# Beacon attention followed by a two-layer MoE block: another order of work in the first two batches

## The chip, the core and the metric

The kernel runs on one core of a Trainium2 chip. Its engines run side by side: TensorE (PE; its weight loads are shown as PEld) multiplies matrices, VectorE (DVE) and ScalarE (ACT) work on elements, GpSimd (POOL) does copies and issues loads, and SyncE (SP) issues loads and stores. Each engine takes its instructions in the order in which they are written, and waits where an operand or a buffer isn't ready. The metric is the device time of one execution in microseconds; lower is better.

## The reference

Eight batches (B), eight heads (H), 576 queries (S) of width 64 (D), and 16 beacon keys in front of the 576 ordinary ones. All queries see the beacon keys; the ordinary keys are causal. The attention output of a batch, heads side by side, gives 576 rows of width 512, and all 4608 rows go through two matrices with a leaky ReLU between them.

```python
k_all = np.concatenate([beacon_k, k], axis=2)
v_all = np.concatenate([beacon_v, v], axis=2)
scores = scale * np.matmul(q, k_all.transpose(0, 1, 3, 2))
causal[:, Nb:] = np.triu(np.ones((S, S), dtype=bool), k=1)
scores = np.where(causal, -1000000000.0, scores)
...
a /= a.sum(-1, keepdims=True) + 1e-09
attn_out = np.matmul(a, v_all)
...
x = attn_out.transpose(0, 2, 1, 3).reshape(B * S, H * D)
h = x @ w_in
g = np.maximum(0.01 * h, h)
out = g @ w_out
```

## The kernel before

**Pairs.** Heads are worked in pairs: four pairs per batch, 32 in all, numbered g = 0 to 31. Each pair has these parts, in this order of need:

- `load_qk(b, grp)` (L124): q and k of two pairs (half a batch), four loads issued by GpSimd, which turn the type to bf16. `permute` (L157) is a copy on GpSimd that brings each 128 x 1152 half into the order that the transposes want. The first pair's own half comes over SP and ACT instead.
- `t_q(g, which)` (L229): nine transposes on TensorE into PSUM (line 244), and one copy out of it (line 249) into qT or kT. For kT a small copy puts the beacon keys in front (L239).
- `score(g, n)` (L256) for n = 0 to 3: the causal blocks of the scores, computed transposed (keys on partitions) into one of two PSUM buffers `sc` (matmuls, L267), and their exponential on ScalarE into `aT` (L278, and L282 for the last block of 80 rows). There are three `aT`, two qT and two kT.
- `masks(g)` (L290): three multiplications on VectorE (L292, L299, L305) that clear the diagonal blocks.
- `value(g, half)` (L314): 12 matmuls for the first three blocks of queries, 18 for the last two (L333); the column of ones in `v_aug` gives the sum. VectorE takes its reciprocal (L342) and multiplies (L343) into `x_nat`.
- `finish(g)` (L488): five transposes of `x_nat` (L355) and a copy into `xT` (L360), which the MoE part reads. After the fourth pair of a batch, one more chunk of 512 rows is ready (`ready`; after the last batch all nine).

**Values.** `load_v(b)` (L207) issues six loads from SP into one of two raw buffers; the first pair's q and k lie in the first of them, so batch 1's values go there once these were read. `cast_v` (L222) turns a batch's values into bf16 in five casts, on VectorE for batches 0 and 1, on GpSimd later. `behind(a, b)` (L199) makes load a wait until load b has landed.

**MoE.** `fill()` (L401) emits the next piece: either `moe1`, four matmuls of 512 columns (L369) with the leaky ReLU on ScalarE (L376), for one of the 16 column blocks of a chunk, or a quarter of `moe2`, four matmuls (L385); after the fourth quarter VectorE copies out (L394) and SP stores. The two kinds take turns where both can run; a chunk's moe2 needs all its 16 moe1. There are 288 fills. If no chunk is ready, `fill()` emits nothing. The weights come in four loads each (`load_w_in`, `load_w_out`, 512 KB each as stored), issued by GpSimd; block i of w_in serves four moe1.

**PSUM.** All tiles other than the scores (transposes, values, MoE accumulators) take turns in four buffers of one tag ("one"), each waiting for the copy out of the tile four before it.

**Order.** The order on every engine is the one written out (`manual_schedule`). The loop over g (L496) emits, per iteration: scores 0 and 1 of pair g, `finish(g - 3)`, `value(g - 2, 0)`, the transposes of pair g + 1, scores 2 and 3 of pair g, `value(g - 2, 1)`, `masks(g)`; so values are two pairs behind scores, and the transposes of x three. Between these stand eight slots for fills: none for g below 6, four for g = 6 and 7, all from g = 9. Iteration 8 is written out apart: it finishes pairs 5 to 7 with fills between, puts 16 fills behind them, and then starts pairs 8 and 9.

Before the loop stand the first loads, the permutes of batch 0, the load of batch 1's q and k behind the last load of v0, and a warm-up of 24 matmuls. The weights are loaded in iteration 3, behind v1. The cast of v0 stands in iteration 2, that of v1 in iteration 5; the transposes of the beacon keys of batches 1 to 7 (L187, which need the cast of `bk` on GpSimd, L178) in iteration 2.

Of the kernel before, what the change touches and what calls it, by code (L numbers as in the profile page):

```python
# [15 lines left out]
def kernel(  # L16
# [11 lines left out]
    nc = tc.nc  # L28

    B, H, S, D = q.shape  # L30
# [5 lines left out]
    NPAIR = H // 2  # L36
# [73 lines left out]
    def load_w_in(i):  # L110
        return nc.gpsimd.dma_start(
            out=w_in_sb[:, :, i * 512 : (i + 1) * 512], in_=w_in_r[:, :, i * 512 : (i + 1) * 512]
        )

    def load_w_out(i):
        return nc.gpsimd.dma_start(
            out=w_out_sb[:, i * 4 : (i + 1) * 4, :], in_=w_out_r[:, i * 4 : (i + 1) * 4, :]
        )
# [5 lines left out]
    def load_qk(b, grp):  # L124


        qk_raw[b, grp] = (
            qkpool.tile([128, 2, RI, D], BF16, name="q_raw"),
            qkpool.tile([128, 2, RI, D], BF16, name="k_raw"),
        )  # L130
        first = None
        for e in range(2):
            if b == 0 and grp == 0 and e == 0:
                continue
            h0 = 4 * grp + 2 * e
            for src, dst in zip((q, k), qk_raw[b, grp]):
                dma = nc.gpsimd.dma_start(  # L137
                    out=dst[e * RP : (e + 1) * RP],
                    in_=src[b, h0 : h0 + 2].rearrange("h (p i) d -> p h i d", i=RI),
                )  # L140
                first = first or dma
        return first
# [14 lines left out]
    def permute(b, grp, which, copy, p0=0, p1=128):  # L157

        if (b, grp) not in nat:
            nat[b, grp] = (  # L160
                natpool.tile([128, RI, 2, D], BF16, name="q_nat"),
                natpool.tile([128, RI, 2, D], BF16, name="k_nat"),
            )
        src, dst = qk_raw[b, grp][which], nat[b, grp][which]
        if b == 0 and grp == 0 and p0 == 0:
            src = first_raw[which]
        copy(out=dst[p0:p1], in_=src[p0:p1].rearrange("p h i d -> p i h d"))  # L167
# [9 lines left out]
    def cast_beacon_k(b0, b1, copy):  # L177
        copy(  # L178
            out=bk[:, b0:b1],
            in_=bk_raw[:, b0:b1, None, :].to_broadcast([128, b1 - b0, 2, D]),  # L180
        )
# [17 lines left out]
    def behind(ins, other):  # L199
        tc.add_manual_dep(  # L200
            ins.ins,
            other.ins.name,
            mybir.DependencyInfo(mybir.DependencyClass.Sync, mybir.DependencyReason.DATA),
            reason="loads in order of need",
        )

    def load_v(b, after=None):  # L207

        t = rawpool.tile([128, NKB, H, D], FP32, name="v_raw")
        v_raws[b] = t  # L210
        first = nc.sync.dma_start(out=t[0:NB, 0], in_=beacon_v[b].rearrange("h p d -> p h d"))
        if after is not None:
            behind(first, after)
        nc.sync.dma_start(out=t[NB:128, 0], in_=v[b, :, 0:112].rearrange("h p d -> p h d"))
        for c in (1, 2, 3, 4):
            last = nc.sync.dma_start(  # L216
                out=t[0 : ROWS[c], c],
                in_=v[b, :, OFF[c] : OFF[c] + ROWS[c]].rearrange("h p d -> p h d"),
            )
        return last  # L220
# [194 lines left out]
    def warm_up(n):  # L415

        ps = ps_one.tile([128, 512], FP32, name="av", tag="one")
        for i in range(n):
            nc.tensor.matmul(out=ps[:, 0:128], lhsT=ident, rhs=ident, start=True, stop=True)

    NG = B * NPAIR

    def has(g):
        return 0 <= g < NG
# [10 lines left out]
    with order:  # L435
        first = load_first_pair()
        load_qk(0, 0)
        make_identity(nc, ident)
        load_qk(0, 1)
        v0 = load_v(0, after=first)  # L440
        load_beacon_k(1, B, nc.sync)
        make_mask()
        make_ones()
        cast_beacon_k(0, 1, nc.scalar.copy)
        permute(0, 0, 0, nc.vector.tensor_copy, 0, RP)
        permute(0, 0, 1, nc.scalar.copy, 0, RP)
        for which in range(2):
            permute(0, 0, which, nc.gpsimd.tensor_copy, RP, 2 * RP)
        for which in range(2):
            permute(0, 1, which, nc.gpsimd.tensor_copy)  # L450
        behind(load_qk(1, 0), v0)
        v1 = load_v(1, after=v0)
        load_qk(1, 1)
        cast_beacon_k(1, B, nc.gpsimd.tensor_copy)
        warm_up(24)
        beacon_transposes(0, 1)
        t_q(0, 0)
        t_q(0, 1, nc.scalar.copy)

        def loads(g):  # L460
            b, hp = divmod(g, NPAIR)
            if g == 1:
                for which in range(2):
                    permute(1, 0, which, nc.gpsimd.tensor_copy)
            elif g == 3:
                for which in range(2):
                    permute(1, 1, which, nc.gpsimd.tensor_copy)
                behind(load_w_in(0), v1)
                for i in range(1, 4):
                    load_w_in(i)  # L470
                for i in range(4):
                    w = load_w_out(i)
                load_v(2, after=w)
                load_qk(2, 0)
                load_qk(2, 1)
            elif b >= 1 and b < B - 1:
                if b > 1:
                    if hp == 0:
                        load_v(b + 1)
                    if hp < 2:  # L480
                        load_qk(b + 1, hp)
                if hp >= 2:
                    for which in range(2):
                        permute(b + 1, hp - 2, which, nc.gpsimd.tensor_copy)
                if hp == 3:
                    cast_v(b + 1, nc.gpsimd)

        def finish(g):  # L488

            x_transposes(g)  # L490
            b, hp = divmod(g, NPAIR)
            if hp == NPAIR - 1:
                ready[0] = NCH if b == B - 1 else b + 1


        for g in range(NG + 3):  # L496
            if has(g):
                loads(g)
            slots = [0] * 8 if g < 6 else [0, 0, 1, 1, 0, 1, 1, 0] if g < 8 else [1] * 8

            def slot(n):
                if slots[n]:
                    fill()

            if g == 2 * NPAIR:

                finish(g - 3)
                value(g - 2, 0)
                fill()
                value(g - 2, 1)  # L510
                fill()
                value(g - 1, 0)
                finish(g - 2)
                value(g - 1, 1)
                fill()
                fill()
                finish(g - 1)
                for n in range(16):
                    fill()
                t_q(g, 0)  # L520
                t_q(g, 1)
                fill()
                fill()
                score(g, 0)
                score(g, 1)
                fill()
                fill()
                fill()
                t_q(g + 1, 0)
                t_q(g + 1, 1)  # L530
                score(g, 2)
                score(g, 3)
                fill()
                fill()
                masks(g)
                fill()
                continue

            late = g - 2 == 2 * NPAIR - 1 or g - 2 == 2 * NPAIR - 2
            if has(g):  # L540
                score(g, 0)
                score(g, 1)
            slot(0)
            if g == 2:
                cast_v(0, nc.vector)
            if g == NPAIR + 1:
                cast_v(1, nc.vector)
            if has(g - 3) and not 2 * NPAIR < g <= 2 * NPAIR + 2:
                finish(g - 3)
            slot(1)  # L550
            if has(g - 2) and not late:
                value(g - 2, 0)
            slot(2)
            slot(3)
            if has(g + 1) and g + 1 != 2 * NPAIR:
                t_q(g + 1, 0)
                t_q(g + 1, 1)
            if has(g):
                score(g, 2)
                score(g, 3)  # L560
            slot(4)
            if has(g - 2) and not late:
                value(g - 2, 1)
            slot(5)
            if g == 2:
                beacon_transposes(1, B)
            slot(6)
            if has(g):
                masks(g)
            slot(7)  # L570
        while done2[0] < NCH * NF:
            fill()

# [29 lines left out]
```

The softmax here doesn't subtract the row's maximum and nothing guards it: scores larger than these inputs give would overflow.

## Time and profile before

| | us |
|---|---|
| median of 13 runs | 379.1 (377.23 to 380.31) |
| profiled execution | 377.35 |
| its span | 375.6 |
| TensorE busy | 352.9 |
| ScalarE busy | 195.6 |
| VectorE busy | 171.4 |
| GpSimd busy | 102.5 |
| scores of pairs 0 to 7 start at | 8.91, 12.30, 15.89, 24.25, 30.48, 34.81, 40.55, 46.91 |
| last x transposes of batch 1 (12 fills done) | 58.50 |

The span is what the profile covers; the execution's own time is 1.75 us longer (377.35 against 375.6). Busy matmuls overlap, so a single matmul of 512 columns is shown with 379 ns, while four of them follow each other within 0.86 us; the starts tell more than the busy time. An arrow in a wait ("<-") names what released the engine. All times in the text count from the start of the span.

### The profile page before, as it was taken

How to read it: one execution, taken by the hardware profiler on the slowest of the kernel's cores; microseconds unless marked ns; L12 is line 12 of the kernel's file. 1: busy time of each engine (PE TensorE's matmuls, PEld its weight loads, DVE VectorE, ACT ScalarE, POOL GpSimd, SP SyncE). 2: the span in 40 equal slices, each digit the busy share in tenths (PEclk: the TensorE clock that was granted, in tenths of full speed). 3: DMA queues.
4: the chain of work that ended last, by engine and by line, in shares of the span. 5: the costliest groups of instructions: out<-in, count | busy, mean ns of one | idle time of the engine just before them, and what ended most of it. 6: DMA issues, size and time to landing. Idle time of an engine off the chain costs nothing.

```text
span 375.6 us, 7668 instructions
## 1 busy us (share of the span) xinstructions
PE 352.9 (94%) x3217; PEld 187.5 (50%) x3264; DVE 171.4 (46%) x402; ACT 195.6 (52%) x308; POOL 102.5 (27%) x143
## 2 busy tenths in 40 slices
PE   4869799999998899999999999999999999999996
PEld 4556464444555455555554555555554554444442
DVE  3768842253558645554456436644554332000021
ACT  3937674376436684368634763487336701643300
POOL 8579216685204812181208202300000000000000
PEclk9999999999999999999999999999999999999999
DMA  8997999959119910178015901100010011001012
GB/s 172 168 201 124 203 201 209 211 106 150 61 61 219 169 24 29 53 133 156 3 58 115 198 2 57 58 2 2 28 58 30 1 45 69 2 0 58 28 56 84
DMA packets 58371, 33.82 MB, mean 90 GB/s; under 512 B 41441, under 2 KB 53473, under 8 KB 58337
## 3 DMA queue, kind: packets, MB, share of 16 engines
q0 software_dynamic: 13152, 13.34, 22.7%
q1 hardware_dynamic: 44896, 19.67, 21.3%
q8 instruction: 25, 0.41, 0.4%
q10 hardware_dynamic: 288, 0.33, 0.3%
q14 instruction: 10, 0.07, 0.1%
HBM read 37.22 MB, written 9.44 MB: 124 GB/s over the span
## 4 chain that ended last, share of the span: by engine, by line
PE 85%; DVE 6%; DMA 3%; POOL 2%; issue 2%; SPq 1%; ACT 0%; POOLq 0%
PE acc L385 33%; PE acc L369 33%; PE av L333 7%; PE sc L267 6%; PE tp L244 4%; PE tp L355 2%; DMA v_raw<-in_k_dram 1%; DMA v_raw<-in_v_dram 1%; DVE osb L394 1%; DVE xT L360 1%; POOL k_raw L137 1%; SPq L216 1%; DVE x_nat L343 1%; DVE qT L249 1%; DVE kT L249 1%
## 5 line engine op out<-in xcount | busy, mean ns | idle before, releaser
L278 ACT ACTIVATE aT<-sc 128x928 bf16<-128x928 f32 (+2 forms) x128 | 102.4, 855 | 76.9 <-PE sc L267 76.7
L369 PE MATMUL acc<-xT,w_in_sb 128*128 128x512 bf16 x551 | 137.7, 379 | 3.5 <-DVE xT L360 2.1
L385 PE MATMUL acc<-w_out_sb,gT 128*128 128x512 bf16 x554 | 135.6, 379 | 1.5 <-issue 0.6
L376 ACT ACTIVATE gT<-acc 128x512 bf16<-128x512 f32 x144 | 85.7, 600 | 80.8 <-PE acc L369 79.6
L385 PEld LDWEIGHTS <-gT 128*128 128x128 bf16 x576 | 52.1, 98 | 60.0 <-issue 5.3
L369 PEld LDWEIGHTS <-w_in_sb 128*128 128x128 bf16 x576 | 52.3, 98 | 59.5 <-issue 4.1
L394 DVE COPY osb<-acc 128x512 f32<-128x512 f32 x36 | 24.8, 690 | 93.4 <-PE acc L385 92.9
L267 PE MATMUL sc<-qT,kT 64*128 64x128 bf16 (+5 forms) x384 | 42.5, 309 | 5.6 <-DVE kT L249 2.8
L333 PEld LDWEIGHTS <-aT 128*128 128x128 bf16 (+1 forms) x960 | 38.8, 100 | 16.7 <-issue 3.3
L333 PE MATMUL av<-v_aug,aT 128*128 128x65 bf16 (+1 forms) x960 | 41.9, 197 | 1.4 <-DVE xT L360 1.0
L167 POOL COPY q_nat<-q_raw 128x1152 bf16<-128x1152 bf16 (+1 forms) x16 | 18.5, 1156 | 82.4 <-PE tp L244 53.6
L249 DVE COPY qT<-tp 128x576 bf16<-128x576 bf16 x32 | 24.2, 755 | 33.0 <-PE tp L244 33.0
L343 DVE TENSOR_TENSOR x_nat<-av,rec 128x384 bf16<-128x384 f32 x64 | 31.4, 491 | 2.2
L225 POOL CAST v_aug<-v_raw 128x512 bf16<-128x512 f32 (+1 forms) x30 | 19.4, 684 | 33.0 <-PE av L333 31.5
L267 PEld LDWEIGHTS <-kT 64*128 64x128 bf16 (+1 forms) x384 | 18.3, 100 | 20.1 <-issue 11.5
L360 DVE COPY xT<-tp 128x576 bf16<-128x576 bf16 x32 | 14.5, 452 | 30.2 <-PE tp L355 30.1
L342 DVE RECIPROCAL rec<-av 128x6 f32<-128x6 f32 x64 | 11.9, 185 | 34.1 <-PE av L333 34.1
L137 POOL DMA_DIRECT2D k_raw<-in_k_dram x31 | 21.2, 683 | 7.8 <-DMA w_out_sb<-in_moe_w_out_dram 4.4
L249 DVE COPY kT<-tp 128x576 bf16<-128x576 bf16 x31 | 23.2, 749 | 0.0
L137 POOL DMA_DIRECT2D q_raw<-in_q_dram x31 | 19.5, 630 | 12.7 <-DMA v_raw<-in_v_dram 4.6
L299 DVE TENSOR_TENSOR aT<-aT,mask 128x768 bf16<-128x768 bf16 x32 | 21.6, 675 | 1.2 <-ACT aT L278 1.2
L167 POOL COPY k_nat<-k_raw 128x1152 bf16<-128x1152 bf16 (+1 forms) x16 | 18.5, 1157 | 1.7 <-DMA k_raw<-in_k_dram 1.5
(33 smaller groups left out, 147.4 us busy)
## 6 DMA issues: line engine op xcount, KB each, us to landing
out_dram<-osb SPq DMA_DIRECT2D x36, 256.0 KB, 2.0
v_raw<-in_v_dram SPq DMA_DIRECT2D x24, 256.0 KB, 6.1
q_raw<-in_q_dram POOLq DMA_DIRECT2D x31, 144.0 KB, 6.1
k_raw<-in_k_dram POOLq DMA_DIRECT2D x31, 144.0 KB, 6.4
w_in_sb<-in_moe_w_in_dram POOLq DMA_DIRECT2D x4, 512.0 KB, 8.6
w_out_sb<-in_moe_w_out_dram POOLq DMA_DIRECT2D x4, 512.0 KB, 16.7
v_raw<-in_v_dram SPq DMA_DIRECT2D x8, 224.0 KB, 4.7
v_raw<-in_v_dram SPq DMA_DIRECT2D x8, 160.0 KB, 4.9
```

The costliest lines, as they stand in the source:

```text
L137: dma = nc.gpsimd.dma_start(out=dst[e * RP : (e + 1) * RP], in_=src[b, h0 : h0 + 2].rearrange("h (p i) d -> p h i d", i=RI),)
L167: copy(out=dst[p0:p1], in_=src[p0:p1].rearrange("p h i d -> p i h d"))
L249: copy(out=dst.rearrange("c (p i) -> c p i", i=RI), in_=ps[:, 0:S].rearrange("c (i p) -> c p i", i=RI),)
L267: nc.tensor.matmul(out=sc[0 : ROWS[c], par, col - c0 : col - c0 + w], lhsT=kT[ps_, c * 128 : c * 128 + ROWS[c]], rhs=qT[ps_, q0 : q0 + w], ...
L278: last = nc.scalar.activation(out=aT[:, :, c0 : c0 + w], in_=sc[:, :, 0:w], func=AF.Exp, scale=0.125)
L299: nc.vector.tensor_tensor(out=diag, in0=diag, in1=tri[:, None, None, :].to_broadcast([128, 2, 3, 128]), op=ALU.mult,)
L333: nc.tensor.matmul(out=avv[:, n, 0 : D + 1], lhsT=aT[0 : ROWS[c], par, a0 : a0 + 128], rhs=va[0 : ROWS[c], c, 2 * hp + par, :], start=(c = ...
L343: nc.vector.tensor_tensor(out=x_nat[:, t0:t1].rearrange("p t e d -> p (t e) d"), in0=avv[:, :, 0:D], in1=rec[:, n0:n1, None].to_broadcast( ...
L369: nc.tensor.matmul(out=acc, lhsT=w_in_sb[:, j, fc * 128 : (fc + 1) * 128], rhs=xT[:, j, i * 512 : (i + 1) * 512], start=(j == 0), stop=(j ...
L376: nc.scalar.activation(out=gT[i][:, fc, :], in_=acc, func=AF.Prelu, alpha=0.01)
L385: nc.tensor.matmul(out=acc, lhsT=gT[i][:, fc, t * 128 : (t + 1) * 128], rhs=w_out_sb[:, fc, :], start=(fc == 0), stop=(fc == NF - 1),)
L394: nc.vector.tensor_copy(out=osb, in_=acc)
```

## The change

The loop is written anew for the first two batches (g < 8):

1. Within iteration g: scores 0 and 1, the transposes of pair g + 1, score 2, `value(g - 1, 0)`, score 3, `value(g - 1, 1)`, `finish(g - 1)`, `masks(g)`. So values follow one pair behind, and `finish` directly behind the values. (In iteration 1 the two halves of value 0 both stand behind score 3.)
2. For odd g the copy of the next pair's kT out of PSUM is on ScalarE.
3. The cast of v0 moves from iteration 2 to 1, that of v1 from iteration 5 to 4. The beacon transposes stay in iteration 2, ahead of the transposes of pair 3.
4. Fills: one at the end of iteration 4, four in each of iterations 5 to 7 (before: four in each of 6 and 7). Iteration 8 finishes pair 7 alone, with three fills ahead of that and 10 instead of 16 behind it.
5. From iteration 9 on the loop has the eight fills as before, but values are one pair behind instead of two, and `finish(g - 1)` stands at the end of the iteration, behind `masks(g)`. The loop ends two iterations sooner.
6. Loads: w_in(0) comes directly behind batch 1's first q and k; v1 waits for the first of these; q and k of pairs 6 and 7 wait for v1; the other weights follow them, ahead of the loop, and v2 behind the last weight. GpSimd permutes pairs 4 and 5 ahead of these waits. The loads of batch 2's q and k stay in iteration 3.

```diff
-        behind(load_qk(1, 0), v0)
-        v1 = load_v(1, after=v0)
-        load_qk(1, 1)
+        gate = load_qk(1, 0)
+        behind(gate, v0)
+        load_w_in(0)
+        v1 = load_v(1, after=gate)
         cast_beacon_k(1, B, nc.gpsimd.tensor_copy)
+        for which in range(2):
+            permute(1, 0, which, nc.gpsimd.tensor_copy)
+        behind(load_qk(1, 1), v1)
+        load_w_in(1)
+        load_w_in(2)
+        load_w_in(3)
+        for i in range(4):
+            w = load_w_out(i)
+        v2 = load_v(2, after=w)
...
         def loads(g):
             b, hp = divmod(g, NPAIR)
-            if g == 1:
-                for which in range(2):
-                    permute(1, 0, which, nc.gpsimd.tensor_copy)
-            elif g == 3:
+            if g == 3:
                 for which in range(2):
                     permute(1, 1, which, nc.gpsimd.tensor_copy)
-                behind(load_w_in(0), v1)
-                for i in range(1, 4):
-                    load_w_in(i)
-                for i in range(4):
-                    w = load_w_out(i)
-                load_v(2, after=w)
                 load_qk(2, 0)
                 load_qk(2, 1)
...
-        for g in range(NG + 3):
+        for g in range(NG + 1):
...
+            if g < 2 * NPAIR:
+
+                moe = g > NPAIR
+                score(g, 0)
+                score(g, 1)
+                if moe:
                     fill()
+                if g + 1 < 2 * NPAIR:
+                    if g + 1 == 3:
+                        beacon_transposes(1, B)
+                    t_q(g + 1, 0)
+                    t_q(g + 1, 1, nc.scalar.copy if g % 2 else nc.vector.tensor_copy)
+                score(g, 2)
+                if g == 1:
+                    cast_v(0, nc.vector)
+                if g == NPAIR:
+                    cast_v(1, nc.vector)
+                if g > 1:
+                    value(g - 1, 0)
+                    if moe:
+                        fill()
+                score(g, 3)
+                if g == 1:
+                    value(0, 0)
+                if g > 0:
+                    value(g - 1, 1)
+                    if moe:
+                        fill()
+                    finish(g - 1)
+                    if g >= NPAIR:
+                        fill()
+                masks(g)
+                continue
 
             if g == 2 * NPAIR:
 
-                finish(g - 3)
-                value(g - 2, 0)
-                fill()
-                value(g - 2, 1)
-                fill()
                 value(g - 1, 0)
-                finish(g - 2)
+                fill()
                 value(g - 1, 1)
                 fill()
                 fill()
                 finish(g - 1)
-                for n in range(16):
+                for n in range(10):
                     fill()
...
-            if has(g - 3) and not 2 * NPAIR < g <= 2 * NPAIR + 2:
-                finish(g - 3)
-            slot(1)
-            if has(g - 2) and not late:
-                value(g - 2, 0)
-            slot(2)
-            slot(3)
-            if has(g + 1) and g + 1 != 2 * NPAIR:
+            fill()
+            fill()
+            if g - 1 >= 2 * NPAIR:
+                value(g - 1, 0)
+            fill()
+            fill()
+            if has(g + 1):
                 t_q(g + 1, 0)
                 t_q(g + 1, 1)
             if has(g):
                 score(g, 2)
                 score(g, 3)
-            slot(4)
-            if has(g - 2) and not late:
-                value(g - 2, 1)
-            slot(5)
...
+            fill()
+            if g - 1 >= 2 * NPAIR:
+                value(g - 1, 1)
+            fill()
+            fill()
             if has(g):
                 masks(g)
-            slot(7)
+            if g - 1 >= 2 * NPAIR:
+                finish(g - 1)
+            fill()
```

More of the change, by code (lines that the diff above doesn't have):

```diff
@@ L493, in finish @@
                 ready[0] = NCH if b == B - 1 else b + 1
-        for g in range(NG + 3):
+        for g in range(NG + 1):
             if has(g):
                 loads(g)
-            slots = [0] * 8 if g < 6 else [0, 0, 1, 1, 0, 1, 1, 0] if g < 8 else [1] * 8
-            def slot(n):
-                if slots[n]:
-                    fill()
+            if g < 2 * NPAIR:
[3 more added lines that the diff above has]
+                if moe:
+                    fill()
+                if g + 1 < 2 * NPAIR:
[24 more added lines that the diff above has]
+                continue
             if g == 2 * NPAIR:
-                finish(g - 3)
-                value(g - 2, 0)
+                value(g - 1, 0)
                 fill()
-                value(g - 2, 1)
-                fill()
-                value(g - 1, 0)
-                finish(g - 2)
                 value(g - 1, 1)
@@ L537 @@
                 continue
-            late = g - 2 == 2 * NPAIR - 1 or g - 2 == 2 * NPAIR - 2
             if has(g):
@@ L542 @@
                 score(g, 1)
[L543 to L547, printed above, removed]
-            if has(g - 3) and not 2 * NPAIR < g <= 2 * NPAIR + 2:
-                finish(g - 3)
-            slot(1)
-            if has(g - 2) and not late:
-                value(g - 2, 0)
-            slot(2)
-            slot(3)
-            if has(g + 1) and g + 1 != 2 * NPAIR:
+            fill()
+            fill()
+            if g - 1 >= 2 * NPAIR:
+                value(g - 1, 0)
+            fill()
+            fill()
+            if has(g + 1):
                 t_q(g + 1, 0)
@@ L560 @@
                 score(g, 3)
-            slot(4)
-            if has(g - 2) and not late:
-                value(g - 2, 1)
-            slot(5)
-            if g == 2:
-                beacon_transposes(1, B)
-            slot(6)
+            fill()
[3 more added lines that the diff above has]
+            fill()
             if has(g):
                 masks(g)
-            slot(7)
+            if g - 1 >= 2 * NPAIR:
+                finish(g - 1)
+            fill()
         while done2[0] < NCH * NF:
```

## The prediction

> **What bounds the kernel now.** I read the page first (busy shares, then the slices), then the stretches of 10 us, the waits of TensorE before 90 us, and the timelines of TensorE, VectorE and GpSimd.
>
> ```profile
> PE 352.9 (94%) x3217; PEld 187.5 (50%) x3264; DVE 171.4 (46%) x402; ACT 195.6 (52%) x308; POOL 102.5 (27%) x143
> ...
> PE   4869799999998899999999999999999999999996
> ```
>
> TensorE is the bound from slice 6 on; only the head and slices 12 and 13 have holes. The stretches show the head and that second hole:
>
> ```profile
> 20.00:30.00 10.00, 7.00 (x87) 5.17 (x85) 6.60 (x16) 4.23 (x6) 6.94 (x10) 1.00 1.09 192
> 30.00:40.00 10.00, 7.39 (x141) 5.51 (x138) 9.20 (x27) 7.72 (x13) 8.41 (x11) 1.00 0.87 138
> ...
> 110.00:120.00 10.00, 9.08 (x138) 5.70 (x138) 7.03 (x17) 5.90 (x8) 2.24 (x2) 1.00 0.88 187
> 120.00:130.00 10.00, 8.35 (x102) 4.74 (x101) 7.11 (x18) 7.21 (x13) 8.62 (x14) 1.00 1.04 181
> ```
>
> After the length, the columns are busy PE, PEld, DVE, ACT, POOL. In the head TensorE isn't only idle, it is slow: nine transposes take
>
> ```profile
> 26.98 0.66 PE L244 MATMUL tp<-ident,q_nat 64*128 64x64 bf16 x9 [0.44 <-POOL q_nat L167]
> ...
> 32.47 0.43 PE L244 MATMUL tp<-ident,q_nat 64*128 64x64 bf16 x9
> ```
>
> and four score matmuls 1.00 at 30.48 and 0.62 at 34.81, so the array turned to full rate near 32 us, after 4 us without a gap (28.1 to 32.1); the clock row doesn't show it. The second hole is a lack of MoE work:
>
> ```profile
> 109.98 0.58 PE L267 MATMUL sc<-qT,kT 64*128 64x512 bf16 x4
> ...
> 123.62 0.38 PE L369 MATMUL acc<-xT,w_in_sb 128*128 128x512 bf16 x1 [1.01 <-DVE xT L360]
> ...
> 131.12 0.59 PE L267 MATMUL sc<-qT,kT 64*128 64x512 bf16 x4
> ```
>
> The scores of pairs 12 and 15 (pair 11's start at 100.17), and between them a first fill that waits for xT. VectorE, and then GpSimd, which the edits load anew:
>
> ```profile
> 36.08 1.96 DVE L225 CAST v_aug<-v_raw 128x512 bf16<-128x512 f32 x5
> ```
>
> ```profile
> 16.05 0.61 POOL L137 DMA_DIRECT2D q_raw<-in_q_dram  x1 [4.61 <-DMA v_raw<-in_v_dram]
> ...
> 22.32 1.01 POOL L178 CAST bk<-bk_raw 128x896 bf16<-128x896 f32 x1
> ```
>
> The casts of v1 are VectorE's longest single block; GpSimd's queue stands still until v0 has landed, and the beacon cast comes behind its loads.
>
> [...] at 37.96 the copy of xT starts as the five casts end, and TensorE had waited 0.97 for it. [...] some 200 GB/s in all from 22 to 29 us with both issuing.
>
> **The change part by part.** Pairs are numbered 0 to 31 over all batches; times of before are starts in the timeline of TensorE. Units at full rate: a fill is 0.8625 (16 matmuls in 3.45 in the chain of waits); a pair's attention 2.91 (9.81 from scores 11 to 12, less 8 fills).
>
> Transposes between score groups: in batch 0 they stood there already. What really moves is the value part, from two pairs behind to one, and the transposes of x, from three behind to directly after the value's second half. They now see the normalization, 0.18 + 0.42 on VectorE with its handovers 0.85, with nothing on TensorE beside it in iterations 1 to 4 (from 5 on a fill of 0.86 stands there and covers it).
>
> *Pairs 0 to 2.* Pair 0 is as before (8.91, 12.30). Pair 1 needs value 0, so the cast of v0, whose last load lands at 16.05: casts end 16.5, value at half rate 0.98 + 1.17 to 18.65, normalization to 19.55, transposes to 20.05. Scores of pair 2 begin there (before 15.89), and end at 21.0. The transposes of the other beacon keys wait for GpSimd's cast: four issues from 16.05 to 20.0, w_in(0) 0.77, cast 1.0, so 21.85. The two stalls of before there (2.06 until 23.38, and 0.49 + 0.44 at pair 4's q and k) nearly vanish: a cover gained, not lost. Then beacon 0.9, q and k 1.0, scores and values 0.5 + 0.98 + 0.5 + 1.15 to 26.95, normalization, transposes: pair 3 starts at 28.3 (before 24.25, with its values two pairs further behind; in work the two are level).
>
> *Pair 3*: scores 0.95, q and k 1.0, 0.5, 1.0, 0.4 to 32.1. I let the array turn to full rate there, as before. 0.57 + 0.85 + 0.3: pair 4 at 33.85.
>
> *Pair 4* is the dearest step. VectorE's queue holds masks(3) to 35.55, qT and kT to 37.1, the five casts of v1 (1.88 start to start) to 38.95, and only then the normalization of value 3, 1.3 for both halves, to 40.25. TensorE finished value 3 at 37.0: 3.3 us idle. Before, the casts cost 0.97 + 1.38. Transposes and one fill (its last matmul waits for xT): pair 5 at 41.45.
>
> *Pairs 5 to 7, with four fills each.* TensorE's own work is 6.2, ScalarE's 3.45 (exponentials) + 4 x 0.5 + 0.55 (kT, pair 5 alone) = 6.0. With both nearly full, the four PSUM buffers bind: the fill behind the value's first half takes the buffer of the fill ahead of the transposes, whose eviction stands behind two exponentials: 0.45. So 48.2, 54.95, 61.0; then 0.7 for masks(7), 0.95 + 0.28 + 3 x 0.8625: the last transposes of batch 1 end at 65.5, with 16 fills done. Before: 58.78 with 12. Four fills are 3.45; head +3.3.
>
> The MoE part of this change is thus 13 fills in iterations 4 to 7 (before 8, in 6 and 7), then 3 instead of 4 ahead of batch 1's last transposes, 10 instead of 16 behind them: no fill is added or lost, only their place moves.
>
> *kT on ScalarE*: three copies (pairs 2, 4, 6) of 0.75 leave VectorE. Two fall where TensorE waits for others: nothing. The one of pair 6 is in the 6.0.
>
> *Loads.* w_in(0) moves ahead of v1, v1 behind the first q of batch 1, q and k of pairs 6, 7 behind v1. Two waits are new. SP's on that first q (3.4 us to landing before, so v1 starts near 19.5 instead of 15.85) has v2 and the outputs behind it, which nobody needs for 30 us. GpSimd's on v1 has all further weights, the permutes of pairs 6, 7 and the next batch's q and k behind it. The same 2.3 MB move from 16 us on at 200 GB/s, so v1 lands near 30 as before. GpSimd then issues four q/k (2.4), three w_in (2.3), four w_out (3.2, the later ones waiting for q/k landings) and permutes (2.3): pairs 6, 7 ready at 40.1; the transposes of pair 6 come at 42.85. Cost nothing, by 2.7 us; beyond that each us costs one. Next batch's q/k queue behind these on GpSimd, but are needed near 74 us. w_in(1) lands near 39, needed at 47. w_out ends near 55, needed after fill 16. v2 on SP follows w_out as before.
>
> *Later.* Before, the stretch from 109.98 to 131.12 is 21.14; its work is 11 fills and 3 pairs, 9.49 + 8.73 = 18.22, so 2.92 lost, since batch 2's last transposes come two iterations late and the 64 fills of two chunks run out. Now 34 fills are done by the end of pair 8, 58 by pair 11, and x of pair 11 is finished in iteration 12 after the 64th: one fill is void, and the next waits for xT some 0.7. Gain 2.2. Bounds: 1.5 (if masks hold xT back) to 3.3 (if the 0.22 at each later batch goes too).
>
> Sum: +3.3 - 2.2, and +0.5 because I put releases at the instant work ends, while the trace has 0.05 to 0.25 from release to start: +1.6. The profiled execution took 377.35 (span 375.6), so 378.95; the median of before stands 1.75 above that execution, so 380.7 in medians. About 0.3% (1.1 us) is what can be told from no change.
>
> **The rivals.** Slower by more (D): [...] Then pair 4 starts 0.85 later, its scores and fill cost 0.5 more, and pair 5 does its first fills at 1.72: together 0.85 + 0.5 + 2.15 (two and a half fills at 0.86 more each) = +3.5, 384.2. For it: 17.4 to 21.3 was dense and released nothing. Against: fills end it at pair 5.
>
> The other side (E), faster: 21.85 to 26.95 is 5.1 us with no gap. If the release comes in it, near 25 us, pairs 2 and 3 run at full rate, pair 4 starts at 31.4 instead of 33.85, pair 5 at 39.2. That is -2.5, so 378.2 with the forecast's later gain and 377.1 with its upper bound; I take 377.7. [...] Beyond it nothing is won: pair 6 isn't ready before 40.1.
>
> (F) Loads come later than reckoned, above 2.7 us: a load waits on the pairs 6 and 7; at 5 us late, +2.3, 383.
>
> **How the numbers follow.** Forecast 0.43 (379 to 382.5), D 0.25, E 0.25, F 0.07. Slower than 380.2: D and F, and over half of the forecast: 0.56. Faster than 378: the larger part of E and a little besides, 0.20. Between: 0.24. Range: 376.6 (E with the later gain and no coupling) to 385.2 (D, 1 us more); outside lie the ends of D and E.
>
> **What would show it.** Nine transposes at 0.43 from 32 us on (forecast), before 27 (E), after 40 (D). TensorE idle some 3 us ahead of pair 3's x transposes, with VectorE's casts beside it. 0.85 ahead of the x transposes of pairs 0 to 2. Last transposes of batch 1 at 65 (63 to 69). Scores 12 to 15 without the hole. If TensorE is idle under 1 us at pair 3's x, or the holes at 110 to 130 stay, the sum is wrong.

## The result, and the profile after

The changed kernel takes 387.75 us (median of 11 runs, 384.03 to 389.72) against 378.75 us (48 runs): ratio 1.0226, interval 1.02 to 1.0252. The forecast was 380.7 us with a range of 376.6 to 385.2, so the sign was right and the size wrong: +1.6 us forecast, +8.6 (2.26% of 378.75) measured. The profiled execution of the changed kernel ("after") took 389.63 (span 387.8), at the upper end of its runs; its times below are its own.

From the page of after, TensorE's busy time, its slices and the granted clock:

```profile
PE 358.0 (92%) x3213; PEld 186.7 (48%) x3264; DVE 167.7 (43%) x399; ACT 196.3 (51%) x311; POOL 100.7 (26%) x143
...
PE   5886699999998899989998999899998999999996
...
PEclk9998699999999899999999999999999999999999
```

Busy time rises by 5.1 us with the same work, which means matmuls that ran slower (on the two pages, 551 of line 369 are busy for 137.7 and 142.0 us), and the clock row shows where: slices 4 and 5, and slice 14, counted from one. The stretches of after give it in numbers (after the length: PE, PEld, DVE, ACT, POOL, then the clock as a share of full rate):

```profile
30.00:40.00 10.00, 7.26 (x78) 3.45 (x78) 6.87 (x20) 5.47 (x9) 7.45 (x9) 0.83 0.51 73
40.00:50.00 10.00, 6.59 (x67) 3.96 (x68) 2.22 (x6) 3.69 (x7) 5.74 (x9) 0.66 1.20 192
110.00:120.00 10.00, 9.94 (x99) 5.20 (x99) 5.55 (x14) 3.47 (x5) 0.00 (x0) 1.00 0.48 119
120.00:130.00 10.00, 7.69 (x72) 3.63 (x72) 5.61 (x11) 3.98 (x6) 8.74 (x13) 0.88 0.74 142
130.00:140.00 10.00, 9.89 (x95) 5.13 (x96) 4.16 (x11) 6.59 (x12) 1.35 (x3) 0.95 0.57 87
```

In these stretches the clock column falls to half where the array is slow throughout (0.50 from 42.9 to 46 us, and 0.50 from 129 to 131), which is called half rate here. By that, 0.83 over 10 us is 3.4 us of half rate, 0.66 is 6.8 us, and 0.88 with 0.95 another 3.4. The hole that before had from 110 us on is gone (9.94 busy from 110 to 120), as forecast. In its place stands a new one at 120 to 130 (7.69). TensorE's waits after 90 us, the first line of the list for before and then for after (line, releaser, us in total, times, longest):

```profile
PE acc L369 <- DVE xT L360: 2.1, 6, 1.0
PE acc L369 <- DVE xT L360: 7.9, 6, 2.2
```

In both, these are six waits of a fill for xT, at the ends of batches 2 to 7. In after they are 2.15, three times 1.49, 1.07 and 0.22. VectorE's timeline at the first of them shows what the fill waits for (start, length, line, out<-in, idle before), with GpSimd's line of the same time last:

```profile
123.54 0.42 DVE L343 TENSOR_TENSOR x_nat<-av,rec 128x256 bf16<-128x256 f32 x1
124.17 0.69 DVE L394 COPY osb<-acc 128x512 f32<-128x512 f32 x1 [0.21 <-DMA out_dram<-osb]
124.78 0.52 DVE L292 TENSOR_TENSOR aT<-aT,mask 128x224 bf16<-128x224 bf16 x1
125.22 0.96 DVE L299 TENSOR_TENSOR aT<-aT,mask 128x768 bf16<-128x768 bf16 x1
126.11 0.69 DVE L305 TENSOR_TENSOR aT<-aT,mask 80x256 bf16<-80x256 bf16 x1
126.72 0.44 DVE L360 COPY xT<-tp 128x576 bf16<-128x576 bf16 x1
...
123.44 3.21 POOL L225 CAST v_aug<-v_raw 128x512 bf16<-128x512 f32 x5
```

TensorE's timeline of after beside it:

```profile
123.97 0.44 PE L355 MATMUL tp<-ident,x_nat 112*128 112x112 bf16 x5
124.25 0.81 PE L369 MATMUL acc<-xT,w_in_sb 128*128 128x512 bf16 x3
127.22 0.38 PE L369 MATMUL acc<-xT,w_in_sb 128*128 128x512 bf16 x1 [2.15 <-DVE xT L360]
```

The x transposes are done at 124.41, but their copy stands behind the copy out of a fill and behind the three masks of the next pair. Of the 2.31 us until it starts, the masks are 1.94 (124.78 to 126.72). Directly after this wait the array ran at half rate: the four score matmuls at 127.53 took 0.96, where those at 51.07 took 0.59.

In the head, TensorE's timeline of after has two waits of that size, each with a half-rate stretch behind it:

```profile
24.69 0.50 PE L355 MATMUL tp<-ident,x_nat 112*128 112x112 bf16 x3
25.62 0.29 PE L355 MATMUL tp<-ident,x_nat 128*128 128x128 bf16 x2 [0.43 <-DVE x_nat L343]
...
35.36 0.95 PE L355 MATMUL tp<-ident,x_nat 112*128 112x112 bf16 x5 [1.92 <-DVE x_nat L343]
...
42.93 0.66 PE L244 MATMUL tp<-ident,q_nat 64*128 64x64 bf16 x9 [3.02 <-POOL q_nat L167]
```

Full rate came near 25 us, as rival E has it: the two transposes at 25.62 took 0.29, where the same two took 0.40 in e1 (at 25.89). It was lost at 35.4 (clock 0.51 from 35.4 to 37 us), behind a wait of 1.92 for VectorE, which had the casts of v1 until 34.61, and again at the q transposes of pair 6 (0.66 for nine, against 0.43 at 52.56). Those waited for GpSimd, whose timeline reads:

```profile
32.55 2.18 POOL L137 DMA_DIRECT2D q_raw<-in_q_dram  x1 [8.61 <-DMA v_raw<-in_v_dram]
...
36.47 2.30 POOL L111 DMA_DIRECT2D w_in_sb<-in_moe_w_in_dram  x3
38.69 3.04 POOL L116 DMA_DIRECT2D w_out_sb<-in_moe_w_out_dram  x4
41.62 1.26 POOL L167 COPY q_nat<-q_raw 128x1152 bf16<-128x1152 bf16 x1
```

The wait for v1 holds seven weight loads and the permutes of pairs 6 and 7 behind it.

The two profiles differ by 12.2 us of span (375.6 and 387.8). The last x transposes of batch 1 start at 68.48 instead of 58.50, with 16 fills done instead of 12: 9.98 - 3.45 = 6.5. The other 5.7 lie after that, and are about the 5.8 more of waiting for xT, with half of the 3.4 us at half rate added and the closed hole taken off.

### The profile page after: what moved, and what is told of

Same layout as the page of the kernel before. It is cut to its first block, busy times and chain, and to the rows that moved or that the text cites. A ratio compares the mean times of both kernels' runs of the same rounds, so it can differ in the third digit from the quotient of the medians.

```text
span 387.8 us, 7663 instructions
## 1 busy us (share of the span) xinstructions
PE 358.0 (92%) x3213; PEld 186.7 (48%) x3264; DVE 167.7 (43%) x399; ACT 196.3 (51%) x311; POOL 100.7 (26%) x143
## 4 chain that ended last, share of the span: by engine, by line
PE 76%; DMA 9%; SPq 6%; DVE 4%; POOL 2%; issue 2%; ACT 1%; POOLq 0%
PE acc L369 31%; PE acc L385 28%; PE av L333 7%; PE sc L267 6%; SPq L216 5%; PE tp L244 4%; DMA out_dram<-osb 3%; DMA v_raw<-in_v_dram 3%; DVE osb L394 2%; PE tp L355 1%; DMA k_raw<-in_k_dram 1%; DMA v_raw<-in_k_dram 1%; DVE aT L299 1%; DMA q_raw<-in_q_dram 1%; ACT aT L278 1%
## 5 line engine op out<-in xcount | busy, mean ns | idle before, releaser
L369 PE MATMUL acc<-xT,w_in_sb 128*128 128x512 bf16 x551 | 142.0, 385 | 9.3 <-DVE xT L360 7.9
L267 PEld LDWEIGHTS <-kT 64*128 64x128 bf16 (+1 forms) x384 | 17.3, 100 | 27.5 <-issue 24.8
L137 POOL DMA_DIRECT2D q_raw<-in_q_dram x31 | 21.1, 680 | 19.8 <-DMA v_raw<-in_v_dram 13.2
L137 POOL DMA_DIRECT2D k_raw<-in_k_dram x31 | 19.6, 631 | 6.3 <-DMA w_out_sb<-in_moe_w_out_dram 3.9
L249 DVE COPY kT<-tp 128x576 bf16<-128x576 bf16 x28 | 20.9, 747 | 0.0
L299 DVE TENSOR_TENSOR aT<-aT,mask 128x768 bf16<-128x768 bf16 x32 | 19.7, 615 | 0.3 <-ACT aT L278 0.3
L244 PEld LDWEIGHTS <-q_nat 64*128 64x128 bf16 x288 | 11.4, 100 | 15.6 <-issue 11.3
L225 POOL CAST v_aug<-v_raw 128x512 bf16<-128x512 f32 (+1 forms) x30 | 18.4, 652 | 1.5 <-DMA v_raw<-in_v_dram 1.3
```

The lines of the kernel that those rows point to most:

```text
L137: dma = nc.gpsimd.dma_start(out=dst[e * RP : (e + 1) * RP], in_=src[b, h0 : h0 + 2].rearrange("h (p i) d -> p h i d", i=RI),)
L244: nc.tensor.transpose(ps[:, i * RP : (i + 1) * RP], nat[b, grp][which][ps_, i].rearrange("p h d -> p (h d)"), ident[ps_, ps_],)
L249: copy(out=dst.rearrange("c (p i) -> c p i", i=RI), in_=ps[:, 0:S].rearrange("c (i p) -> c p i", i=RI),)
L267: nc.tensor.matmul(out=sc[0 : ROWS[c], par, col - c0 : col - c0 + w], lhsT=kT[ps_, c * 128 : c * 128 + ROWS[c]], rhs=qT[ps_, q0 : q0 + w], ...
L299: nc.vector.tensor_tensor(out=diag, in0=diag, in1=tri[:, None, None, :].to_broadcast([128, 2, 3, 128]), op=ALU.mult,)
L369: nc.tensor.matmul(out=acc, lhsT=w_in_sb[:, j, fc * 128 : (fc + 1) * 128], rhs=xT[:, j, i * 512 : (i + 1) * 512], start=(j == 0), stop=(j ...
```

## The experiments

Times are medians; ratios are to the kernel before, run beside it on the same chip, whose median was 378.03 (e1 to e4), 379.2 (e5 to e8), 378.33 (e9 to e11) and 379.25 (e12). The head means the iterations up to g = 8, the later loop those from g = 9.

**e1: the x transposes ahead of the masks in the later loop.** The changed kernel with two statements exchanged.

```diff
+            if g - 1 >= 2 * NPAIR:
+                finish(g - 1)
             if has(g):
                 masks(g)
-            if g - 1 >= 2 * NPAIR:
-                finish(g - 1)
             fill()
```

> The changed kernel; from iteration 9 on the x transposes and their copy stand ahead of the masks on VectorE instead of behind them. Theory (the later loss of 5.7 us is the fill that waits for xT behind the masks at each end of a batch, 7.9 us in six waits against 2.1 before, and the half-rate stretch that the first one brings): the six waits fall to about 2, the half-rate stretch at 128 us goes, 6 to 7 us gained: 381 against 387.75. Rival (VectorE is simply late there, because GpSimd casts the next values beside it and masks take 0.96 instead of 0.55): the masks now come later, values wait for them instead, under 2 us gained: 386.

379.19 us, ratio 1.0023 (0.9992 to 1.0055). VectorE's timeline of e1 at the same batch end:

```profile
120.29 0.69 DVE L394 COPY osb<-acc 128x512 f32<-128x512 f32 x1 [0.21 <-DMA out_dram<-osb]
120.89 0.45 DVE L360 COPY xT<-tp 128x576 bf16<-128x576 bf16 x1
121.26 0.72 DVE L292 TENSOR_TENSOR aT<-aT,mask 128x224 bf16<-128x224 bf16 x1
121.90 0.96 DVE L299 TENSOR_TENSOR aT<-aT,mask 128x768 bf16<-128x768 bf16 x1
```

and the waits of TensorE after 90 us in e1:

```profile
PE acc L369 <- DVE xT L360: 1.3, 6, 0.2
```

Two of the masks are as slow as in after, but TensorE doesn't wait for them. Two statements take back 0.0203 of the ratio, 7.7 us, which is nearly all of the loss.

**e4 and e5: the later loop alone.** The kernel before with its later loop replaced by that of the change (e4), and then with the exchange of e1 as well (e5).

> The kernel before with only the loop from iteration 9 on as changed (values one pair behind, x transposes behind the masks); the first nine iterations and all loads as before. Theory (the loop from iteration 9 on alone costs some 5.7 us): 384 against 378.75, waits for xT near 7.9 us. Rival (that loss comes only from what the changed head leaves behind, fills and loads out of step): 377, the hole at 110 to 124 us gone and nothing lost.

> The kernel before with the loop from iteration 9 on as changed, but the x transposes and their copy ahead of the masks. Theory (the changed loop loses by that order alone, and without it its shorter lag closes the hole at 110 to 124 us as the prediction had it): 2 to 2.5 us less than before, 375.8 against 378.0. Rival (the gain in the earlier swap came from a head that happened to run well): no better than before, 378 or more.

e4: 385.2 us, 1.0182 (1.0118 to 1.0246). e5: 377.47 us, 0.9959 (0.9939 to 0.9979). TensorE's waits after 90 us in e4:

```profile
PE acc L369 <- DVE xT L360: 7.2, 6, 1.5
PE tp L355 <- DVE x_nat L343: 1.1, 1, 1.1
```

and in e5:

```profile
PE tp L355 <- DVE x_nat L343: 1.1, 1, 1.1
PE acc L369 <- DVE xT L360: 1.1, 5, 0.2
```

So the later part costs 6.9 us as written, with the head of before in front of it, and gains 1.6 us once the order is turned: the order is worth some 8.4 us (0.0223 of the ratio).

**e7: the head alone.** The changed loads and first nine iterations, with the later loop of before.

> The changed kernel with only its loads and its first nine iterations; from iteration 9 on the loop of before (values two pairs behind, x transposes three). Theory (the changed head costs 2 to 3 us, and up to 6.5 where the array falls back to half rate in it; the hole of before stays): 381, between before and the changed kernel. Rival (the head carries most of the 9 us): 385 or more.

384.27 us, 1.014 (1.0112 to 1.0168), +5.3 us. This later loop still has its hole, now at the array's cost too: TensorE's timeline of e7 has

```profile
125.83 0.20 PE L333 MATMUL av<-v_aug,aT 80*128 80x65 bf16 x1
127.32 0.94 PE L267 MATMUL sc<-qT,kT 64*128 64x512 bf16 x4 [1.29 <-DVE kT L249]
```

with four score matmuls in 0.94 where they take 0.59 at full rate. So e7 lies between its two theories, and the parts don't add up: 6.9 + 5.3 is 12.2, the whole change 8.6. The half-rate stretch behind that wait (clock 0.87 and 0.96 in the two stretches from 120 us) is worth 1.7 us; where the rest comes from isn't shown.

**e9 and e8: GpSimd's cast taken away from the masks.** In after GpSimd casts the next values from 123.44 to 126.65, exactly beside the three slow masks. e9 has the masks still ahead of xT, but lets the cast wait for the copy of xT. e8 tried the same by a fourth buffer for the permuted halves, so that GpSimd would be free earlier.

```diff
-                if hp == 3:
-                    cast_v(b + 1, nc.gpsimd)
...
-            x_transposes(g)
+            last = x_transposes(g)
...
+                if 1 <= b < B - 1:
+                    cast_v(b + 1, nc.gpsimd, last)
```

> The changed kernel with one edit: from the third batch on, GpSimd's cast of the next values waits until VectorE has copied the batch's last x transposes, so that the three masks ahead of that copy run with GpSimd's cast out of the way; their order is left as it is. Theory that half of the six waits for xT comes from the masks being slowed beside the cast (0.52, 0.96 and 0.69 us where they otherwise take 0.27, 0.55 and 0.28): masks back at 0.55, the six waits down from 7.9 to near 5 us, no half-rate stretch at the batch end, 384.5 us (2.5 to 4 us less than 387.75). Theory that the order alone makes the wait: the same waits, 387.0 to 387.8 us. Slower than 388 if the later cast makes the values late for the next batch, with a wait of the first values on V behind it.

> The changed kernel with four instead of three buffers for permuted q and k, so that GpSimd's permutes and its cast of the next values are through before a batch ends and no longer run beside the masks there. Theory of the order (xT behind the masks): masks become shorter, the six waits fall by some 0.6 each, 2 to 4 us gained at most: 385. Rival (GpSimd's cast beside VectorE is the cause): the waits fall to those of before, 381 or less. If masks were slow for another reason: 387.75.

e9: 385.5 us, 1.0178 (1.0143 to 1.0214). VectorE's timeline of e9 (lines two further on):

```profile
124.50 0.69 DVE L396 COPY osb<-acc 128x512 f32<-128x512 f32 x1 [0.22 <-PE acc L387]
125.11 0.27 DVE L294 TENSOR_TENSOR aT<-aT,mask 128x224 bf16<-128x224 bf16 x1
125.29 0.55 DVE L301 TENSOR_TENSOR aT<-aT,mask 128x768 bf16<-128x768 bf16 x1
125.76 0.28 DVE L307 TENSOR_TENSOR aT<-aT,mask 80x256 bf16<-80x256 bf16 x1
125.96 0.45 DVE L362 COPY xT<-tp 128x576 bf16<-128x576 bf16 x1
...
126.47 2.85 POOL L225 CAST v_aug<-v_raw 128x512 bf16<-128x512 f32 x5 [37.88 <-DVE xT L362]
```

and its waits after 90 us:

```profile
PE acc L371 <- DVE xT L362: 5.6, 6, 1.1
```

The masks take 0.85 start to start instead of 1.94, and the waits fall by 2.3 us, as does the median (387.75 to 385.5; the intervals of the two ratios overlap, so that gain in time is likely rather than shown). e1, with the order turned, waits 1.3, so of the 6.6 us between 7.9 and 1.3 the cast beside the masks is 2.3, about a third, and the order the larger part. e8 doesn't test it: its cast still stands beside the masks (118.84 to 122.05), because there it waits for values on TensorE, as the profile has it, and not for a permuted half, and its waits for xT are 7.5 in all. It is all the same faster than the change, with intervals that don't overlap: 385.18 us, 1.0145 (1.0108 to 1.0182). In its profile batch 1's last x transposes start at 64.05 instead of 68.48. With so few runs, whether the buffer did that isn't shown.

Which of VectorE's instructions are longer beside the cast can be read from the two timelines: the masks (aT and mask) take 0.27, 0.55 and 0.28 in e9, and 0.52, 0.96 and 0.69 in after beside the cast, while the osb copy takes 0.69 in both. Why the masks are the ones isn't shown.

**e3 and e10: idle matmuls in the waits of the head.** The change with 30 idle matmuls ahead of the x transposes of pair 3 and 44 ahead of the q transposes of pair 6; and e5 with 50 in three places of its head.

```diff
+                    if g == 5:
+                        warm_up(44)
...
+                    if g == 4:
+                        warm_up(30)
                     finish(g - 1)
```

> The changed kernel with 30 idle matmuls of 128 columns ahead of the x transposes of pair 3 and 44 ahead of the q transposes of pair 6, where TensorE waits 1.9 and 3.0 us anyway; no wait is taken away. Theory (a wait of some 2 us costs more than itself, since the array falls back to half rate and the 6 us of work behind pair 6's transposes then run at half): 2.5 to 3.5 us gained: 384.7, and no half-rate stretch between 35 and 49 us. Rival (behind the wait ScalarE and VectorE set the pace): within 1 us of 387.75.

> The first head of the kernel before with the changed later loop and its x transposes ahead of the masks, to which idle matmuls are added (results unused): 18 before the transposes of the beacons in the third iteration, 32 around the values of the fourth pair. [...] full rate from about 25 us in place of 32, and some 2 us less than without the idle matmuls (375.5 against 377.5 us). Theory that VectorE and the arriving data pace the first pairs: no change, 377 to 378 us, with longer waits in place of the slower matmuls.

That idle matmuls bring or hold full rate was the author's estimate. e3: 387.03 us, 1.0226 (1.0165 to 1.0286). Its clock held (0.98 and 1.00 in the stretches from 30 and 40 us, against 0.83 and 0.66), and batch 1's last x transposes started at 66.14 instead of 68.48, but the time isn't told from that of the change without them. That the idle matmuls held the clock isn't shown either: the profile of e1, with the same head and none of them, held it too, and finished batch 1 earlier (64.59). e10: 377.12 us, 0.9962 (0.9943 to 0.9981), against 0.9959 for e5: no change. In its profile full rate did come early, near 23.8 us, where seven beacon transposes took 0.56 instead of 0.93, but it was lost again behind a wait of 1.29 for kT (30.28; clock 0.92 and 0.70 in the stretches from 25 and 30 us) that no idle matmul filled, so a head at full rate throughout wasn't tried. Neither run got faster by the idle matmuls; that VectorE, GpSimd and the data set the pace of the first pairs fits this, but isn't shown by it.

**e2, e6, e11, e12: the loads, and the casts of v1.** e2 is the change with the loads and permutes of before. e6 is that with the exchange of e1. e11 is e6 with the casts of v1 moved behind pair 3's normalization, and e12 the same with the new loads.

```diff
-                if g == NPAIR:
-                    cast_v(1, nc.vector)
...
                     finish(g - 1)
+                    if g == NPAIR:
+                        cast_v(1, nc.vector)
```

> The changed kernel with the loads and permutes as before (q and k of pairs 4 to 7 together behind v0, weights behind v1). Theory (the head loses because q and k of pairs 6 and 7 are permuted at 42.9 and 44 us, behind v1 and all weight issues, and the array falls back to half rate while it waits): the waits of 3.0 and 0.4 go, the half-rate stretch from 42 to 49 us shrinks to nothing, against a beacon cast that comes 2 us later: 4 to 6 us gained, 382.5. Rival (the order of values and x transposes and ScalarE's load bind pairs 4 to 7, the loads are hidden): under 1.5 us gained: 386.5.

> The changed kernel with both: loads and permutes as before, and the x transposes ahead of the masks from iteration 9 on. Theory (the new order of loads costs some 1.5 us of the head, on top of the order of values): 377.6, against 379.2 with the swap alone. Rival (the head is bound by the normalization ahead of the x transposes and by ScalarE, loads are hidden): 379.2.

> The changed kernel with the loads of the kernel before and the x transposes ahead of the masks, to which one edit is added: VectorE's casts of the second batch's first values stand behind the normalization and x copy of pair 3 instead of ahead of it. Theory that these casts, 1.6 us, make the 1.9 us wait of the x transposes of pair 3 and the fall of the clock after it: that wait gone, full rate kept to the end of the second batch, some 2 us less than 378.4 us (376.5). Theory that the wait only moves to the values of pair 4, which need the casts: 378 to 379 us, the wait now at the values of pair 4 or 5.

> The changed kernel, its own loads kept, with both orders turned: the x transposes ahead of the masks from the third batch on, and the casts of the second batch's first values behind the normalization of pair 3. It stands to the run with the loads of the kernel before (376.69 us, 0.9946) as new loads to old. Theory that GpSimd's wait for the values of batch 1 makes the second half of that batch late, and costs about 1.5 us: 378 us (ratio 0.998), with a wait of 1.5 to 3 us for the permuted q of pair 6 near 42 us. Rival, as forecast, that the new loads cost nothing: 376.5 to 377 us, with a wait there under 1 us.

| run | loads | casts of v1 | x ahead of masks | us | ratio (interval) |
|---|---|---|---|---|---|
| after | new | early | no | 387.75 | 1.0226 (1.02 to 1.0252) |
| e2 | before's | early | no | 386.15 | 1.0217 (1.0154 to 1.0279) |
| e1 | new | early | yes | 379.19 | 1.0023 (0.9992 to 1.0055) |
| e6 | before's | early | yes | 378.43 | 0.9992 (0.9964 to 1.0019) |
| e12 | new | late | yes | 379.88 | 1.0027 (1.0008 to 1.0046) |
| e11 | before's | late | yes | 376.69 | 0.9946 (0.9921 to 0.9971) |

TensorE's timeline of e12 at pair 6:

```profile
37.34 1.04 PE L369 MATMUL acc<-xT,w_in_sb 128*128 128x512 bf16 x4
41.52 0.66 PE L244 MATMUL tp<-ident,q_nat 64*128 64x64 bf16 x9 [3.15 <-POOL q_nat L167]
```

and of e11:

```profile
40.32 1.04 PE L369 MATMUL acc<-xT,w_in_sb 128*128 128x512 bf16 x4
41.29 0.43 PE L244 MATMUL tp<-ident,q_nat 64*128 64x64 bf16 x9
```

With the casts of v1 early, as in the change, the loads of before gain nothing that can be told: 0.0009 from after to e2, whose theory had 4 to 6 us, and 0.0031 from e1 to e6, with intervals that overlap. With the casts late, the new loads cost 0.0081 of the ratio, 3.1 us, in a wait of 3.15 at the place where the forecast had 2.7 us to spare; twice what e12's first theory expected, since after the wait the array ran at half rate again (clock 0.66 from 40 to 50 us). Moving the casts seems to gain 0.0046, 1.7 us, with the loads of before (e6 to e11); the intervals just overlap. With the new loads it gains nothing (e1 to e12). There the permuted halves come late either way (the q transposes of pair 6 start at 41.68 and 41.52), which is the likely reason. e11, e5 and e10 are the fastest versions, faster than both kernels; they can't be told apart.

## Why the prediction was wrong

**"Later", the step that failed.** The forecast had -2.2 us, with bounds of 1.5 to 3.3 of gain; the later loop alone measured +6.9 (e4). Its reason was right: the hole is gone, and with the order turned the loop gains 1.6 (e5). The term that was mis-sized is "the next waits for xT some 0.7". It was put in once, for the first batch end, and its bound "if masks hold xT back" gave it 0.7 more. In the profile of after it is 7.9 us over six batch ends. Two things were left out. The longer wait recurs at every batch end with masks ahead of xT, since the first fill of a new chunk always needs the pair just finished; the forecast knew a wait of 0.22 at each later batch end, and let it stay or go, but not grow. And VectorE's queue holds a copy of 0.69 and three masks ahead of xT. The masks take 1.94 at the first of these waits, beside GpSimd's cast, and 0.85 in e9 without it. For pair 4 the forecast had walked through VectorE's queue step by step; here it didn't. e1 shows that the order makes the loss, e9 that without the cast 5.6 of the 7.9 remain. Half rate after the longest wait adds to it in this profile. The 0.0203 of the ratio that the exchange gives back is most of the 2.26%. So most of the loss comes from part 5 of the change, and not from the first two batches that the title names.

**Loads: "Cost nothing, by 2.7 us".** The times were wrong; the cost of nothing isn't refuted for the kernel as changed (after and e2, e1 and e6), but it is 3.1 us once the casts are out of the way (e11 and e12). Pairs 6 and 7 were to be ready at 40.1; the permute of q began at 41.62, and that of k ended near 44. v1 landed at 32.5 rather than near 30, and the first issue behind it took 2.18 instead of 0.61. That issue ends at 34.73, as VectorE's casts of v1 end (34.61). In before it was the same: the second issue took 2.19 from 16.64 and ended at 18.83, as VectorE's casts of v0 end (18.72). In e12 and e1, where no cast stood beside it, the same issue took 0.61. But in e12 the casts ran beside the four issues of w_out and were themselves the slower ones (3.33 instead of 1.76 in after), so either side can be the longer one. Why, no run isolated. Rival F named this wait, at 0.07, as a small risk.

**Head, +3.3.** Measured +5.3 with before's later loop (e7), and +2.4 from e5 to e1, where the later loop is the same (0.0064 of the ratio). In the profile of e1, whose array came to full rate near 36 us (the forecast assumed 32; two transposes took 0.40 at 31.57 and 0.28 at 38.25) and kept it (nine in 0.43 at 41.68, clock 1.00 from 40 to 70 us), batch 1's last x transposes end at 65.03 against 65.5 forecast. That agreement is partly luck: pairs 2 to 5 started 1.6 to 2.1 us early there, and waits of 0.73 and 0.72 for q and k of pair 6, which the forecast had at nothing, took most of it back. In that of after, with an earlier release, they end at 68.92. There the scores of pairs 2 to 5 started at 18.17, 25.84, 30.11 and 37.94 against 20.05, 28.3, 33.85 and 41.45 forecast, all early, through rival E's release and an earlier pair 2. Iteration 5 then took 13.1 us instead of 6.75: 3.4 of waiting for q and k, and 6.8 us at half rate. From pair 6 (51.07) to pair 7 (57.94) is 6.87 against 6.75: the balance of TensorE and ScalarE was right. "Pair 4 is the dearest step" was right in kind, with 1.92 idle instead of 3.3, and worth some 1.7 us where nothing else is late (e6 to e11).

**The rivals.** E was right about the release and wrong about its worth. Pair 5 started 3.5 us early; of these, 2.1 are in e1 too, without the release, and all of it ended at pair 6, as E's last sentence says. D, with full rate only in pair 5, did not hold in this profile. When full rate comes, and with it the odds of D and E, was the author's estimate; the traces don't show what brings it. All of them treated full rate as something gained once. That the array can fall back after a wait (1.29 us in e7, 2.15 in after) was in no case.

What stays open is when the array is released. With the same head it came near 25 us in the profile of after and near 36 us in that of e1, which nevertheless finished batch 1 earlier. No run set this at will, and only one execution of each kernel is profiled. The mean clock of the other runs of after is known, from 0.959 to 0.994, though that figure can miss half rate at the start. The time doesn't follow it: 384.06 and 389.72 us both have 0.981. A slip in the reading of before is without weight: counted from one, its second hole is in slices 13 and 14.

## What to carry to other kernels

When a stage is moved, read the queue of every engine that serves it at the new place: the copy that the next matmul needs must stand ahead of work with slack (here some 8.4 us, by the ratios of e4 and e5). A wait found at one batch end has to be multiplied by all the batch ends, and priced with the operations ahead of it in the queue, each at the length that it has beside its new neighbours (the three masks 1.94 us in after, 0.85 in e9). A load made to wait holds up everything behind it on its queue (in after 8.61 us, with seven weight loads and two permutes behind it), so put loads that are needed soon ahead of the wait.

## What was unexpected in the hardware

The forecast treated full rate as something that stays. Half rate followed waits of 1.92, 3.02 and 2.15 us in after, and of 1.29 us in e7. But the length of the wait doesn't decide alone: three waits of 1.49 us at later batch ends of after left the clock as it was (1.00 from 169.75, the first, to 180 us, with seven fill matmuls in 1.68), and so did 1.98 us in e8 (122.61; clock 1.00 from 120 to 140 us) and 2.16 us in e2 (clock 1.00 there too), at the same batch end where after lost it:

```profile
124.07 0.38 PE L369 MATMUL acc<-xT,w_in_sb 128*128 128x512 bf16 x1 [2.16 <-DVE xT L360]
124.38 0.59 PE L267 MATMUL sc<-qT,kT 64*128 64x512 bf16 x4
124.90 1.90 PE L369 MATMUL acc<-xT,w_in_sb 128*128 128x512 bf16 x8
```

These are lines of e2; in after the eight matmuls behind the same wait took 3.17. What decides wasn't found. The stretches of after lasted 3.4 or 6.8 us by the clock column. Where the array does fall back for 3.4 us, half of them, 1.7 us, is an estimate of what the wait costs in slow matmuls beyond its own length.

The clock column doesn't always show the array's start at half rate: in after it reads 1.00 from 20 to 30 us, though three transposes took 0.50 at 24.69 and 0.34 at 29.07, so that the array was at half rate up to about 25; in e11 it reads 0.50 from 20 to 30 us, where nine transposes took 0.68 (28.40).
